# An earlier first weight chunk and moved conversions in a windowed-attention and two-MLP kernel

## The chip, the cores and the metric

The kernel runs on one core of one Trainium2 chip. The time is device microseconds of one execution, from launch to end. The kernel before took 948.12 us (median of 3 runs, 947.3 to 948.22). Five engines work side by side, each through its own instruction queue in order: TensorE (PE, with weight loads as PEld), VectorE (DVE), ScalarE (ACT), GpSimd (POOL) and SyncE (SP), which here only issues transfers. They wait for each other through semaphores.

## The reference

```python
# attention: q, k, v are (4, 8, 576, 64) f32; window 128, causal, ALiBi slopes per head
scores = (1 / sqrt(64)) * q @ k.T
mask = (rel >= 0) & (rel < 128)                 # rel = query position - key position
scores = where(mask, scores - slope[h] * abs(rel), -1e9)
attn = softmax(scores)                          # row sum + 1e-9 in the denominator
x = (attn @ v) with the heads of a token side by side      # (2304, 512)
# first MLP: w_in (512, 2048) and w_out (2048, 512), both float64
h = x @ w_in
g = where(h >= 1, h, where(h <= -1, 0, (h + 1)**2 / 4))
x = g @ w_out
# second MLP, same shapes, float64 weights
h = x @ w_in2
out = (h * clip(h + 3, 0, 6) / 6) @ w_out2
```

## The kernel before, in words

**Stages.** The 2304 tokens are cut into attention units of 64 to 256 tokens (`units`). A unit has 8 heads, and a head one or two blocks of up to 128 queries; one block of one head is a *step*. The first unit has 256 tokens, so 16 steps. The first MLP runs over blocks of 256 or 384 tokens and over 16 chunks of the hidden dimension (`f`), the second MLP after it. Attention steps of later units are dealt out between the first MLP's chunks; the first unit's run alone, ahead of everything.

**A step.** `Attention.tick` (L601) runs one step's stages at lags: `stage_a` (L414) makes the scores on TensorE (`s`, L411), VectorE takes bias, mask and row minimum (L441), and ScalarE the exponential (L445, `p` and `sm`). Two ticks later `stage_b` transposes on TensorE (`t`, L469 and L470) and ScalarE copies (`tt`). Three ticks later `stage_c_whole` multiplies with the values (`r`, L506). After both heads of a pair VectorE divides (`rec`, `y`, L518 to L520); a tick later `stage_d_whole` transposes (L531), ScalarE casts the chunk of `x` and VectorE writes its remainder (L152 and L159, both helper lines). A pair of heads gives one of the four 128-row chunks of x; the first MLP's hidden products (`h`, L655) need all four. `h` goes through VectorE (L684), ScalarE (L685), VectorE (L686), a cast on ScalarE (`g`, L152) and a remainder on GpSimd (`g`, L159) before `acc` (L697) can use it.

**Weights.** A chunk `f` of the float64 weights comes in two transfers of 512 KB, w_in and w_out (`Weights.load`, L172: one of the two each time it is called), into `rawa<f>`. It is turned into a pair of f32 tiles in three parts (L189 to L220): `conv1` has ScalarE on the two 32-bit halves (L194 and L198) and GpSimd on the sign (L197); `conv2` puts the parts together on VectorE (L205 and L212, both with two inputs in SBUF); `conv3` casts on ScalarE (`wa`, L152) and takes the remainder on VectorE (`wa`, L159). `conv_tick` (L222) emits `conv2` and `conv3` of chunk n-1 and then `conv1` of chunk n. The first hidden products of chunk f need `wa` of that chunk.

**Order.** SyncE's order is that of the program text. TensorE, VectorE, ScalarE and GpSimd are ordered when the program is built, by a scheduler that works with its own estimates; `tc.issue_after(i)` makes it put what is emitted inside behind instruction i, and `att.behind()` (L630) does so with the last step's row minimum. The pre-phase (L859 to L865) runs `n_pre` = 20 ticks: 16 of the first unit and four of lag, in which the first steps of the second unit start. Its only weight work are one load at every even tick and four calls of `conv_tick`, at t = 9, 14, 18 and 19. The first MLP then starts, with a hook per chunk (`spread`, L867) that calls one load, the conversions that are due, and the attention steps that are due.

Of the kernel before, what the change touches and what calls it, by code (L numbers as in the profile page):

```python
# [15 lines left out]
AF = mybir.ActivationFunctionType  # L16
# [17 lines left out]
LAG_B, LAG_C, LAG_D = 2, 3, 4  # L34
LAG_B_SPLIT, LAG_C_SPLIT = 3, 5
WARM_UP = 6
WHOLE = 4


@with_exitstack  # L40
def tile_window_attention_two_mlps(
# [15 lines left out]
    nc = tc.nc  # L57
# [190 lines left out]
    for j, (t0, n) in enumerate(units):  # L248
        for h in range(H):
# [9 lines left out]
            u.p = {}  # L259
            u.whole = j < WHOLE  # L260
            u.n_a = u.n_c = 0
# [8 lines left out]
    class Attention:  # L270
# [143 lines left out]
        def stage_a(self, n, i):  # L414
# [4 lines left out]
            nk = a + m - ks  # L419
# [9 lines left out]
            pt = self.pt[self.n_p % ((LAG_B if u.whole else LAG_B_SPLIT) + 1)]  # L429
            self.n_p += 1  # L430
            sm = self.work.tile([P, 4], F32, tag="sm", name=f"sm{n}_{i}", bufs=4)
# [3 lines left out]
            if not u.whole and a >= P:  # L435
# [3 lines left out]
                nk, table = P, self.near  # L439

            self.row = nc.vector.tensor_tensor_reduce(  # L441
                out=pt[:, :nk], in0=ps[:, :nk], in1=table,
                scale=-scale if u.whole else -slopes[u.h],
                scalar=3.0e38, op0=ALU.add, op1=ALU.min, accum_out=sm[:, 0:1])
            nc.scalar.activation(out=pt[:, :nk], in_=pt[:, :nk], func=AF.Exp, bias=sm[:, 0:1],  # L445
                                 scale=-1.0, accum_out=None if u.whole else sm[:, 1:2])
            if not u.whole:
                nc.vector.tensor_scalar(out=sm[:, 2:3], in0=sm[:, 1:2], scalar1=EPS, scalar2=None, op0=ALU.add)  # L448
# [152 lines left out]
        def tick(self):  # L601
            t = self.t
            self.t += 1
            first, whole = unit_steps[0], sum(unit_steps[:WHOLE])
            for lag, span, stage in ((LAG_D, range(first), self.stage_d_whole),
                                     (LAG_D + 1, range(first, whole), self.stage_d_whole),
                                     (LAG_C, range(whole), self.stage_c_whole),
                                     (LAG_C_SPLIT, range(whole, len(steps)), self.stage_c),
                                     (LAG_B, range(whole), self.stage_b),
                                     (LAG_B_SPLIT, range(whole, len(steps)), self.stage_b)):  # L610
                if t - lag in span:
                    stage(*steps[t - lag])
            if t < len(steps):
                n, i = steps[t]
                u = heads[n]
                self.more_loads(n + 3)
                self.more_preps(n)
                self.stage_a(n, i)
                late, self.late = self.late, []
                with self.behind():  # L620
                    for x in late:
                        self.to_x(*x)
                    if i == 0:
                        self.more_preps(n + 1 if u.whole or len(u.qbs) > 1 else n + 2)
                self.more_loads(n + 3)
            else:
                while self.late:
                    self.to_x(*self.late.pop(0))

        def behind(self):  # L630


            return tc.issue_after(self.row.ins) if self.row else ExitStack()
# [186 lines left out]
    W1 = Weights("a", w_in1, w_out1, cpool, True)  # L820
# [16 lines left out]
    with ExitStack() as actx:  # L837
# [6 lines left out]
        att = Attention(raw, proc, work, XX)  # L844
# [5 lines left out]
        bank = psum.tile([P, BANK], F32, tag="h1", name="busy")  # L850
        for _ in range(WARM_UP):
            keep_busy(bank, BANK)
# [2 lines left out]
            nc.gpsimd.memset(vt[:, :, 0:2 * D + 2:2 * D + 1], 1.0)  # L855
        att.more_loads(1)
        W1.load()

        n_pre = unit_steps[0] + LAG_D  # L859
        for t in range(n_pre):  # L860
            att.tick()
            if t % 2 == 0:
                W1.load()
            if t in (n_pre // 2 - 1, n_pre - 6) or t >= n_pre - 2:
                W1.conv_tick()  # L865

        def spread(part, ticks, conv):  # L867

# [467 lines left out]
```

## Time and profile before

| | us |
|---|---|
| median of 3 runs | 948.12 (947.3 to 948.22) |
| the profiled execution | 946.91 |
| its span, from the first to the last instruction | 945.2 |

| engine | busy us | share of the span | instructions |
|---|---|---|---|
| PE | 928.9 | 98% | 5683 |
| PEld | 875.2 | 93% | 5683 |
| DVE | 659.8 | 70% | 1750 |
| ACT | 535.4 | 57% | 1349 |
| POOL | 306.1 | 32% | 575 |

A line of the timeline gives an instruction's start and duration; the next instruction of the same engine can start some tenths of a microsecond before the one ahead has ended, so the start of the next one tells better what an instruction costs its engine. Matmuls overlap too, so a TensorE that reads as busy can still issue fewer matmuls than it could: the count in a stretch (x) says more. In square brackets stands how long the engine sat idle before the instruction and who ended it. Shares are averages over the whole program, whose first 60 us differ much from the rest.

### The profile page before, as it was taken

Reading aid. Unit: us, or ns where it says so; the run is one execution under the profiler, and the core shown is the slowest. Engines: PE = TensorE matmul, PEld = TensorE weight load, DVE = VectorE, ACT = ScalarE, POOL = GpSimd, SP = SyncE. Lnnn points to the kernel's source line nnn. Section 1 sums busy time; section 2 is a strip of 40 time slices with the busy share of each in tenths; the row PEclk is TensorE's granted clock in tenths of the full one; section 3 lists DMA queues with packets and bytes.
Section 4 is the critical chain, followed back from the end, with each engine's and each line's share of the span. In section 5 each row is a group of like instructions: output and inputs, shape, how many; then the busy total and the mean of one; then the engine's idle time right before and its main releaser. Section 6 shows DMA issues by size and latency. Waiting matters only on the chain.

```text
span 945.2 us, 17238 instructions
## 1 busy us (share of the span) xinstructions
PE 928.9 (98%) x5683; PEld 875.2 (93%) x5683; DVE 659.8 (70%) x1750; ACT 535.4 (57%) x1349; POOL 306.1 (32%) x575
## 2 busy tenths in 40 slices
PE   8899999999999999999999999999999999999998
PEld 6799999999999999999999999999999898888987
DVE  6998975786677677767647989848557777644443
ACT  6998854676667566666636876425333334423233
POOL 3243844787668676777710000000000000000000
PEclk9999999999999999999999999999999999999999
DMA  8858332232222212322007880004264644543441
GB/s 258 238 170 271 107 93 88 68 86 68 73 61 76 77 47 62 88 76 61 3 34 251 298 276 22 1 23 167 79 211 167 235 171 151 169 123 112 122 113 67
DMA packets 95337, 114.90 MB, mean 122 GB/s; under 512 B 8848, under 2 KB 73616, under 8 KB 95248
## 3 DMA queue, kind: packets, MB, share of 16 engines
q1 hardware_dynamic: 95248, 113.80, 38.2%
q8 instruction: 45, 0.74, 0.3%
q14 instruction: 44, 0.36, 0.1%
HBM read 88.60 MB, written 25.17 MB: 120 GB/s over the span
## 4 chain that ended last, share of the span: by engine, by line
PE 85%; DVE 6%; DMA 3%; ACT 3%; issue 1%; POOL 1%; SPq 0%; ACTq 0%; POOLq 0%; DVEq 0%
PE h L655 25%; PE acc L756 21%; PE acc L697 17%; PE y L1237 7%; PE x L1237 5%; PE s L411 3%; PE r L554 3%; DMA rawa<-w_out 2%; PE t L470 2%; PE r L506 1%; DMA rawa<-w_in 1%; DVE kl L391 1%; DVE r L684 1%; DVE r L686 1%; DMA qw<-qT 1%
## 5 line engine op out<-in xcount | busy, mean ns | idle before, releaser
L655 PE MATMUL h<-x,wa 128*128 128x384 f32 (+1 forms) x1344 | 231.0, 317 | 1.2 <-DVE r L686 0.8
L697 PE MATMUL acc<-g,wa 128*128 128x384 f32 (+1 forms) x1344 | 227.7, 315 | 0.4 <-POOL g L159 0.4
L756 PE MATMUL acc<-wb,g 128*128 128x512 f32 x861 | 222.2, 393 | 0.0
L655 PEld LDWEIGHTS h<-x,wa 128*128 128x128 f32 x1344 | 206.6, 189 | 4.3 <-DVE r L686 3.1
L697 PEld LDWEIGHTS acc<-g,wa 128*128 128x128 f32 x1344 | 206.2, 189 | 1.0 <-POOL g L159 0.6
L756 PEld LDWEIGHTS acc<-wb,g 128*128 128x128 f32 x861 | 159.4, 188 | 24.9
L152 ACT CAST g<-r 128x384 fp32r<-128x384 f32 (+1 forms) x208 | 101.3, 487 | 70.4 <-DVE r L1184 37.6
L159 POOL TENSOR_TENSOR g<-r,g 128x256 fp32r<-128x256 f32 (+1 forms) x96 | 93.4, 973 | 67.5 <-ACT g L152 51.4
L685 ACT ACTIVATE r<-r 128x384 f32<-128x384 f32 (+1 forms) x112 | 53.5, 478 | 80.4 <-DVE r L684 79.8
L159 DVE TENSOR_TENSOR g<-r,g 128x384 fp32r<-128x384 f32 x112 | 62.4, 557 | 43.2 <-ACT g L152 42.8
L684 DVE TENSOR_SCALAR r<-h 128x384 f32<-128x384 f32 (+1 forms) x112 | 55.4, 495 | 45.0 <-PE h L655 38.2
L488 POOL TENSOR_SCALAR_AFFINE_SELECT tt<-dist 128x256 fp32r<-128x256 f32 (+1 forms) x176 | 76.5, 455 | 14.0 <-DVE dist L483 13.9
L686 DVE TENSOR_TENSOR r<-h,r 128x384 f32<-128x384 f32 (+1 forms) x112 | 55.8, 499 | 27.9 <-ACT r L685 26.1
L655 PE MATMUL h<-x,wb 128*128 128x384 f32 x384 | 72.5, 336 | 0.0
L655 PEld LDWEIGHTS h<-x,wb 128*128 128x128 f32 x384 | 68.2, 188 | 2.6
L445 ACT ACTIVATE p<-p,sm 128x128 f32<-128x128 f32 (+2 forms) x134 | 57.0, 427 | 21.0 <-DVE sm L441 20.8
L1182 ACT ACTIVATE r<-u 128x384 f32<-128x384 f32 x32 | 16.8, 526 | 56.5 <-DVE u L1246 56.5
L554 PEld LDWEIGHTS r<-tt,vs 128*128 128x128 f32 x304 | 44.7, 189 | 3.1 <-issue 1.4
L393 POOL TENSOR_TENSOR qs<-qr,qs 128x256 fp32r<-128x256 f32 (+2 forms) x64 | 39.4, 616 | 25.1 <-ACT qs L390 13.3
L554 PE MATMUL r<-tt,vs 128*128 128x128 f32 (+3 forms) x304 | 44.3, 262 | 1.3 <-POOL tt L488 0.9
L470 PE MATMUL t<-ident,p 128*128 128x128 f32 x134 | 38.4, 288 | 1.0 <-DVE sm L448 0.5
L391 DVE SCALAR_TENSOR_TENSOR kl<-kr,kh 128x256 fp32r<-128x256 f32 (+3 forms) x64 | 38.9, 608 | 0.0
(161 smaller groups left out, 1553.6 us busy)
## 6 DMA issues: line engine op xcount, KB each, us to landing
w<-wd SPq DMA_DIRECT2D x88, 256.0 KB, 2.7
rawa<-w_in SPq DMA_DIRECT2D x16, 512.0 KB, 5.2
rawa<-w_out SPq DMA_DIRECT2D x16, 512.0 KB, 5.4
rawb<-w_in SPq DMA_DIRECT2D x16, 512.0 KB, 3.9
rawb<-w_out SPq DMA_DIRECT2D x16, 512.0 KB, 4.9
wd<-sum SPq DMA_DIRECT2D x32, 256.0 KB, 2.2
wd<-wb SPq DMA_DIRECT2D x24, 256.0 KB, 2.8
out<-o SPq DMA_DIRECT2D x17, 256.0 KB, 2.2
```

Source lines behind the costliest of these rows:

```text
L152: nc.scalar.copy(hi, x)
L159: engines[eng].tensor_tensor(out=lo, in0=x, in1=hi.bitcast(F32), op=ALU.subtract)
L445: nc.scalar.activation(out=pt[:, :nk], in_=pt[:, :nk], func=AF.Exp, bias=sm[:, 0:1], scale=-1.0, accum_out=None if u.whole else sm[:, 1:2])
L470: nc.tensor.transpose(ps[:, 1, :], pt[:, P:] if u.whole and has_prev else pt[:, :P], ident)
L488: nc.gpsimd.affine_select(out=u.tt[:, :, s0 + s, :m], in_=both, compare_op=ALU.is_ge, fill=0.0, base=-1 + s, pattern=[[0, 2], [sign, m]], ...
L554: nc.tensor.matmul(u.r[:, qo:qo + nq], u.vs[:, j, c, :, :].rearrange("p a d -> p (a d)"), u.tt[:, part].rearrange("p s q -> p (s q)")[:, s ...
L655: nc.tensor.matmul(ps[:, :n], self.W.w_in(a, c, f), self.x_chunk(x, b, c, n), start=(k == 0), stop=(k == 3 * KC - 1))
L684: nc.vector.tensor_scalar(out=r[:, :n], in0=ps[:, :n], scalar1=-1.0, scalar2=1.0, op0=ALU.max, op1=ALU.min)
L686: nc.vector.tensor_tensor(out=r[:, :n], in0=ps[:, :n], in1=r[:, :n], op=ALU.max)
L697: nc.tensor.matmul(acc[i][:, o * n:(o + 1) * n], self.W.w_out(a, f)[:, e * P:(e + 1) * P], g[:, b, :n], start=(first and k == 0 and o == 0 ...
L756: nc.tensor.matmul(acc[t][:, :DM], g[:, b, tg * P:(tg + 1) * P], self.W.w_out(a, f), start=(first and k == 0), stop=(last and k == 2))
L1237: nc.tensor.matmul(ps[:, :N2], w[:, a, c * P:(c + 1) * P], self.x.operand(k, c, b), start=(start and n == 0), stop=(n == 5), skip_group_ch ...
```

## The change

There are two parts. In front of the pre-phase `W1.load()` is called twice, not once, so the second half of chunk 0 is asked for right behind the first; each load of the pre-phase and of the hooks after it is then one transfer further than before. And the four calls of `conv_tick` stand at t = 4, 10, 15 and 19 in place of 9, 14, 18 and 19, inside a context that queues everything that they emit behind the last step's row minimum and its exponential.

```diff
--- before.py
+++ after.py
@@ -34,6 +34,7 @@
 LAG_B, LAG_C, LAG_D = 2, 3, 4
 LAG_B_SPLIT, LAG_C_SPLIT = 3, 5
 WARM_UP = 6
+CONV_AT = 4, 10, 15, 19
 WHOLE = 4
 
 
@@ -442,7 +443,7 @@
                 out=pt[:, :nk], in0=ps[:, :nk], in1=table,
                 scale=-scale if u.whole else -slopes[u.h],
                 scalar=3.0e38, op0=ALU.add, op1=ALU.min, accum_out=sm[:, 0:1])
-            nc.scalar.activation(out=pt[:, :nk], in_=pt[:, :nk], func=AF.Exp, bias=sm[:, 0:1],
+            self.exp = nc.scalar.activation(out=pt[:, :nk], in_=pt[:, :nk], func=AF.Exp, bias=sm[:, 0:1],
                                  scale=-1.0, accum_out=None if u.whole else sm[:, 1:2])
             if not u.whole:
                 nc.vector.tensor_scalar(out=sm[:, 2:3], in0=sm[:, 1:2], scalar1=EPS, scalar2=None, op0=ALU.add)
@@ -627,6 +628,9 @@
                 while self.late:
                     self.to_x(*self.late.pop(0))
 
+        def behind_exp(self):
+            return tc.issue_after(self.exp.ins)
+
         def behind(self):
 
 
@@ -855,14 +859,16 @@
             nc.gpsimd.memset(vt[:, :, 0:2 * D + 2:2 * D + 1], 1.0)
         att.more_loads(1)
         W1.load()
+        W1.load()
 
         n_pre = unit_steps[0] + LAG_D
         for t in range(n_pre):
             att.tick()
             if t % 2 == 0:
                 W1.load()
-            if t in (n_pre // 2 - 1, n_pre - 6) or t >= n_pre - 2:
-                W1.conv_tick()
+            if t in CONV_AT:
+                with att.behind(), att.behind_exp():
+                    W1.conv_tick()
 
         def spread(part, ticks, conv):
 
```

SyncE's queue behind the first weight transfer, before. `kw` is a head's k, `qw` a pair's q, `vr` a pair's v, `rawa0` weight chunk 0; the first pair's loads stand ahead of these rows.

```order
L182 DMA rawa0_169<-w_in1 128x4x256
L315 DMA kw1_106<-kT 64x256
L317 DMA qw0_107<-qT 128x256
L315 DMA kw1_106<-kT 64x256
L327 DMA vr1_103<-v 128x2x128
L186 DMA rawa0_169<-w_out1 128x1024
L315 DMA kw_kh0_109<-kT 64x256
L317 DMA qw1_108<-qT 128x256
L315 DMA kw_kh1_110<-kT 64x256
L327 DMA vr2_104<-v 128x2x128
L182 DMA rawa1_202<-w_in1 128x4x256
```

The same place after the change.

```order
L183 DMA rawa0_169<-w_in1 128x4x256
L187 DMA rawa0_169<-w_out1 128x1024
L316 DMA kw1_106<-kT 64x256
L318 DMA qw0_107<-qT 128x256
L316 DMA kw1_106<-kT 64x256
L328 DMA vr1_103<-v 128x2x128
L183 DMA rawa1_182<-w_in1 128x4x256
L316 DMA kw_kh0_109<-kT 64x256
L318 DMA qw1_108<-qT 128x256
L316 DMA kw_kh1_110<-kT 64x256
L328 DMA vr2_104<-v 128x2x128
```

The second half of chunk 0 went ahead of the second pair's k, q and v, and the first half of chunk 1 ahead of the third pair's; every later pair stands behind one more weight transfer in the same way.

ScalarE's queue from the exponential of step 4 on, before. `sm2_0` names head 2, block 0; `tt` are the copies of transposed probabilities, `x1` the cast of the first x chunk, `ma0` and `rawa0` the conversion of chunk 0.

```order
L445 ACTIVATE p1_114<-p1_114,sm2_0_225 128x128
L445 ACTIVATE p2_115<-p2_115,sm2_1_237 128x256
L445 ACTIVATE p0_113<-p0_113,sm3_0_258 128x128
L152 COPY tt2_247<-t2_0_248 128x128
L152 COPY tt2_247<-t2_1_270 128x256
L445 ACTIVATE p1_114<-p1_114,sm3_1_277 128x256
L152 CAST x_78<-x1_263 128x256
L194 ACTIVATE ma0_304<-rawa0_169 128x1024
L152 COPY tt3_282<-t3_0_283 128x128
L152 COPY tt3_282<-t3_1_294 128x256
L445 ACTIVATE p2_115<-p2_115,sm4_0_289 128x128
L198 ACTIVATE rawa0_169<-rawa0_169 128x1024
```

After the change.

```order
L446 ACTIVATE p1_114<-p1_114,sm2_0_226 128x128
L195 ACTIVATE ma0_231<-rawa0_169 128x1024
L199 ACTIVATE rawa0_169<-rawa0_169 128x1024
L446 ACTIVATE p2_115<-p2_115,sm2_1_243 128x256
L153 COPY tt2_253<-t2_0_254 128x128
L446 ACTIVATE p0_113<-p0_113,sm3_0_264 128x128
L153 COPY tt2_253<-t2_1_275 128x256
L153 CAST x_78<-x1_268 128x256
L446 ACTIVATE p1_114<-p1_114,sm3_1_282 128x256
L446 ACTIVATE p2_115<-p2_115,sm4_0_294 128x128
L153 COPY tt3_287<-t3_0_288 128x128
L446 ACTIVATE p0_113<-p0_113,sm4_1_307 128x256
```

Both conversion instructions of chunk 0 now stand next to each other right behind the exponential of head 2's first block, ahead of that of its second block; before, they stood seven and eleven places behind it. When ScalarE's queue comes to the exponential of head 8's first block (`sm8_0`), the same instructions stand ahead of it in both programs.

ScalarE's queue a little later, up to the cast of the fourth chunk of x (`x7`), before.

```order
L152 COPY tt8_450<-t8_0_451 128x256
L152 COPY tt8_450<-t8_1_483 128x256
L194 ACTIVATE ma3_497<-rawa3_329 128x1024
L445 ACTIVATE p0_113<-p0_113,sm9_0_461 128x256
L152 CAST wa2_494<-ma2_471 128x1024
L152 CAST x_78<-x7_475 128x256
L445 ACTIVATE p1_114<-p1_114,sm9_1_489 128x256
L198 ACTIVATE rawa3_329<-rawa3_329 128x1024
```

After the change.

```order
L153 COPY tt8_461<-t8_0_462 128x256
L153 COPY tt8_461<-t8_1_484 128x256
L446 ACTIVATE p0_113<-p0_113,sm9_0_472 128x256
L153 CAST x_78<-x7_476 128x256
L446 ACTIVATE p1_114<-p1_114,sm9_1_490 128x256
L195 ACTIVATE ma3_498<-rawa3_297 128x1024
L199 ACTIVATE rawa3_297<-rawa3_297 128x1024
L195 ACTIVATE ma4_529<-rawa4_370 128x1024
L153 CAST wa2_495<-ma2_427 128x1024
```

The cast of x7 and the exponentials of head 9 now stand ahead of chunk 3's first conversion (`ma3`) and of the cast of chunk 2 (`wa2`), which stood ahead of them before; behind them three conversion instructions stand in a row.

## Rows read from the trace of the kernel before

**Rows 1.** Busy time by stretch of 20 us; columns in the first line.
```profile
core 0: us, PE busy (x) PEld busy (x) DVE busy (x) ACT busy (x) POOL busy (x), PEclk, DMA share, GB/s
0.00:20.00 20.00, 16.39 (x104) 12.40 (x105) 11.73 (x45) 12.13 (x30) 6.12 (x22) 1.00 0.85 249
20.00:40.00 20.00, 16.01 (x110) 13.46 (x109) 17.69 (x41) 18.43 (x33) 6.85 (x7) 1.00 1.01 291
40.00:60.00 20.00, 19.36 (x148) 18.11 (x148) 19.32 (x48) 18.83 (x40) 6.88 (x8) 1.00 0.38 118
60.00:80.00 20.00, 20.00 (x171) 19.93 (x171) 17.31 (x52) 18.85 (x41) 9.77 (x17) 1.00 0.72 221
```

**Rows 2.** SyncE's timeline, 4 to 10 us: start us, duration us, then the transfer issued.
```profile
4.34 0.59 SPq L317 DMA_DIRECT2D qw<-qT  x1
...
6.12 0.47 SPq L186 DMA_DIRECT2D rawa<-w_out  x1
...
7.15 0.58 SPq L317 DMA_DIRECT2D qw<-qT  x1
...
9.44 0.50 SPq L186 DMA_DIRECT2D rawa<-w_out  x1
```

**Rows 3.** Transfers issued 3.3 to 6.5 us: count, size, us from issue to landing.
```profile
rawa<-w_out SPq DMA_DIRECT2D x1, 512.0 KB, 5.5
...
qw<-qT SPq DMA_DIRECT2D x1, 128.0 KB, 4.0
```

**Rows 4.** The same for transfers issued 6.7 to 9.9 us.
```profile
rawa<-w_out SPq DMA_DIRECT2D x1, 512.0 KB, 7.1
...
qw<-qT SPq DMA_DIRECT2D x1, 128.0 KB, 5.0
```

**Rows 5.** TensorE's timeline, 9.5 to 14.3 us: start us, duration us, instruction.
```profile
10.04 1.09 PE L411 MATMUL s<-kw,qw 128*128 128x128 f32 x6
...
13.73 0.39 PE L411 MATMUL s<-kw_kh,qw 128*128 128x128 f32 x2
```

**Rows 6.** VectorE's timeline, 10 to 11.2 us.
```profile
10.65 0.42 DVE L520 TENSOR_TENSOR y<-r,rec 128x256 f32<-128x256 f32 x1
10.99 0.28 DVE L441 CUSTOM_DVE_ANT_0 p<-s,dist 128x128 f32<-128x128 f32 x1
```

**Rows 7.** ScalarE's timeline, 11 to 39 us.
```profile
11.31 1.15 ACT L445 ACTIVATE p<-p,sm 128x128 f32<-128x128 f32 x3 [1.82 <-DVE sm L441]
...
13.62 1.15 ACT L194 ACTIVATE ma<-rawa 128x1024 f32<-128x1024 f32 x1
14.66 0.54 ACT L152 COPY tt<-t 128x128 f32<-128x128 f32 x2
...
15.38 1.19 ACT L198 ACTIVATE rawa<-rawa 128x1024 int32<-128x1024 uint32 x1
...
17.74 0.40 ACT L445 ACTIVATE p<-p,sm 128x128 f32<-128x128 f32 x1
...
28.38 0.54 ACT L445 ACTIVATE p<-p,sm 128x256 f32<-128x256 f32 x1
...
33.48 0.40 ACT L152 CAST x<-x 128x256 fp32r<-128x256 f32 x1
...
38.74 0.40 ACT L152 CAST g<-r 128x256 fp32r<-128x256 f32 x1
```

**Rows 8.** Busy time in two stretches, with the columns of rows 1.
```profile
11.31:18.05 6.74, 6.14 (x40) 4.36 (x39) 4.21 (x18) 6.28 (x16) 1.13 (x1) 1.00 1.06 322
18.05:38.74 20.69, 16.43 (x110) 13.62 (x111) 18.21 (x44) 18.74 (x35) 6.08 (x6) 1.00 1.00 288
```

**Rows 9.** VectorE's timeline, 42 to 52 us: one conversion step, twice.
```profile
42.86 1.22 DVE L212 CUSTOM_DVE_ANT_0 ma<-rawa,ma 128x2048 uint16<-128x2048 uint16 x1
...
49.29 2.17 DVE L212 CUSTOM_DVE_ANT_0 ma<-rawa,ma 128x2048 uint16<-128x2048 uint16 x1
```

**Rows 10.** GpSimd's timeline, 42 to 53 us.
```profile
49.26 1.15 POOL L197 TENSOR_SCALAR rawa<-rawa 128x1024 f32<-128x1024 f32 x1 [3.47 <-ACT ma L194]
```

## The prediction

> **What bounds the kernel now.** I read the busy time by stretch first. From 60 us on TensorE issues 171 matmuls in 20 us and is never idle; before that it issues 104, 110 and 148 [rows 1]. The first 20 us hold short padding matmuls and the start, so the stretches to look at are 20 to 40 (61 too few, at 20/171 = 0.117 us each some 7.1 us) and 40 to 60 (23, some 2.7 us). All that an edit of the start can win lies there, since afterwards TensorE sets the pace. In those 40 us ScalarE is busy for 18.43 + 18.83 = 37.26 us, VectorE for 37.01, and the transfers are saturated until 40 us (DMA share 0.85 and 1.01) [rows 1]. So the first 60 us belong to ScalarE and VectorE, who share attention steps and weight conversions, and behind them to the transfers. Second, SyncE's issues with the times to landing say when data is there [rows 2 to 4]; third, the timelines say who waited for it [rows 5 to 7].
>
> **The loads.** Before, the second half of chunk 0 lands at 6.12 + 5.5 = 11.6 us, q of the second pair at 4.34 + 4.0 = 8.3, q of the third at 7.15 + 5.0 = 12.15, the second half of chunk 1 at 9.44 + 7.1 = 16.5 [rows 2 to 4]. Transfers land in the order of issue and the engines are full, so bytes that are moved ahead delay those behind by their own time: 512 KB (0.524 MB) take 1.6 us at the 322 GB/s of a busy stretch [rows 8] and 2.1 at the 249 of the first [rows 1], in which this lies. I take 2.0. The second half of chunk 0 then lands near 9.8 us. The second pair's q lands at 10.4; its score matmul ran at 10.04 [rows 5], so it is 0.4 us late, but the row minimum behind it waited until VectorE had made y at 10.65 and started at 10.99 [rows 6]: hidden. The third pair's q lands near 14.15 and its scores ran at 13.73 [rows 5]: 0.4 us late, and its exponential is not due before 15.6 in the new order (below): hidden too, by ScalarE. If that cover were gone, the cost would be up to 0.6 us. Chunk 1 is complete at 16.6 as before, because the moved bytes are all ahead of it either way, and its conversion starts after that.
>
> **The conversions on ScalarE.** A long conversion instruction costs 14.66 - 13.62 = 1.04 us of ScalarE's queue [rows 7]. Chunk 0 would be there at 9.8, but its conversion is queued behind the exponential of step 4, which starts at 11.31 [rows 7] in both programs: the idle time ahead of 11.31 (1.82 us in that row) stays idle. The pair of conversions runs from 11.62 to 13.70, 2 us earlier than the first of them did (13.62), and the exponentials, copies and the first cast of x, which filled 11.62 to 13.62, follow it. What can be gained is ScalarE's idle time: 6.74 - 6.28 = 0.46 us between 11.31 and 18.05, and 20.69 - 18.74 = 1.95 between 18.05 and 38.74 [rows 8], 2.4 in all. I followed the new queue instruction by instruction with the durations of the trace. New waits appear, because the two or three engines of a step answer each other with less in flight: 0.5 us ahead of the exponential of head 4's second block, 0.8 ahead of the last copy of head 5, 0.35 ahead of head 8's copies, 0.65 ahead of the cast of x7, which comes to 2.3. So the queue is neither ahead nor behind: the exponential of head 5's first block ends at 17.6, where before two more copies (0.43 us) had been done by 18.05; and the exponential of head 8, with the same instructions ahead of it, starts at 28.3 (before 28.38 [rows 7]).
>
> **The fourth chunk of x.** From there the order differs in a way that helps. The first conversion of chunk 3 and the cast of chunk 2 (1.04 + 0.95 = 2.0 us) no longer stand ahead of the cast of x7, which moves from 33.48 [rows 7] to about 31.5. The first chunk's hidden products can end 2 us earlier. But its g does not come 2 us earlier: three conversion instructions now stand between, and I find its cast at 38.2 against 38.74 [rows 7], 0.54 us earlier, with 0.24 us more of other work done by then.
>
> **VectorE beside GpSimd.** The same conversion step took 1.22 us alone and 2.17 us where GpSimd's sign instruction began at the same time [rows 9, 10]. In the new order the sign instruction of chunk n starts when ScalarE has done the first conversion of chunk n, about when VectorE comes to that step of chunk n-1: near 18.7, 26.0 and 33.2 us. Each meeting costs VectorE between 0 and 0.95 us. VectorE was idle for 27.43 - 22.42 = 5.0 us of these two stretches [rows 8], which hides most; the one near 26 us delays the cast of chunk 1 by 0.5. The Trainium skill says the same under GPSIMD Engine Reference, section Specifications: GpSimd shares its SBUF interfaces with VectorE, with contention for VectorE instructions with two SBUF inputs, as this step is. By that rule all three meetings are paid in full, 2.85 us on VectorE, and if half a microsecond of each came through, the forecast would be 948.5 us.
>
> **The sum.** Loads 0; the earlier conversion 0; ScalarE's idle time 2.4 less new waits 2.3, within the next term; g earlier by 0.54 and 0.24 of work, 0.8; VectorE's meetings 0 to -0.8, taken as -0.3. That is -0.5 us. Later hooks call the same conversions at the same places, and the orders come together again within the first MLP's first blocks, so I carry the shift to the end unchanged. The profiled execution took 946.91 us (span 945.2), which becomes 946.4; the median of the runs lies 1.2 above it, so the forecast is 947.6 us. What a measurement can tell from no change is about 0.2%, 1.9 us: faster means below 946.2, slower above 950.0.
>
> **Rivals.**
> - *Faster: TensorE takes all of x7.* If the first hidden products end 2 us earlier and the later ones follow, the 7.1 us of missing matmuls shrink by that much and 0.5: 948.1 - 2.5 = 945.6, and up to 4 us if the new waits on ScalarE don't show. For it: hidden products are what TensorE lacks. Against: g's chain runs through ScalarE, which has the same work to do.
> - *Slower: the pair of conversions delays the first unit.* Two conversions, 2.08 us, stand ahead of the exponential of step 5, and each later step needs its answer from TensorE and VectorE. If ScalarE doesn't run back to back from 13.7 us on, that 2.08 us goes through to x7 and the first g, together with a late third pair: 948.1 + 2.1 = 950.2, to 951.5 with the 0.6 of the loads and VectorE's meetings. It decides from the point where the cast of x7 starts after 34.5. Against: ScalarE was idle for only 0.46 of the 6.74 us of that stretch [rows 8], so it had work in hand there.
> - *Nothing: it does not do what it says.* Chunk 0 is converted earlier, but chunk 1's tick is only one step earlier and the last tick is the same, so 2 us of head start end in the 40 to 60 us stretch, where ScalarE and VectorE are 94 and 97% busy [rows 1]: 948.1 to 949.
>
> **How the numbers follow.** Forecast 0.37 (its own range 946.4 to 948.6), nothing 0.16, faster 0.29 (943.9 to 946.2), slower 0.18 (949 to 951.5, a sixth of it under 950.0). Faster by over 0.2%: 0.29; within: 0.37 + 0.16 + 0.03 = 0.56; slower: 0.15. The range reaches into both outer cases and leaves out about a tenth at each end: 944.7 to 950.4.
>
> **What would show it.** SyncE's second transfer of chunk 0 landing before 10 us; ScalarE's pair of conversions at 11.6 to 13.7 right behind one exponential; the scores of the third pair near 14.3; the exponential of head 8 near 28.3; the cast of x7 near 31.5; the first g's cast near 38.2; VectorE's step at over 1.5 us near 18 or 26 us. The forecast is wrong if x7 comes at 31.5 or sooner and g's cast before 37.5 (faster), or if x7 comes after 33.5 (slower), or if stretches beyond 60 us, where I change nothing, issue another number of matmuls.

## The result, and the profile after

The changed kernel is slower: 957.49 us, median of 4 runs (955.86 to 958.02), where the kernel before took 947.87 on the same chip (947.3 to 948.22). The ratio is 1.0101 with a 95% interval of 1.0088 to 1.0113. The profiled execution took 957.05 us, its span 955.3, 10.1 more than before.

In the rows of after the line numbers are one higher as far as the attention goes (the conversions at L195 and L199 for L194 and L198, the helper at L153 for L152) and four higher in the MLP (L659 for L655). First the busy time by stretch, with the columns of [rows 1]; the last line is a stretch that rows 1 doesn't have.

```profile
0.00:20.00 20.00, 15.75 (x95) 12.31 (x95) 9.83 (x40) 11.32 (x27) 6.10 (x23) 1.00 0.91 270
20.00:40.00 20.00, 14.52 (x99) 11.70 (x97) 16.45 (x42) 17.34 (x34) 7.74 (x6) 1.00 0.92 272
40.00:60.00 20.00, 19.00 (x133) 17.53 (x133) 16.92 (x39) 17.38 (x36) 7.04 (x6) 0.91 0.42 134
60.00:80.00 20.00, 19.34 (x155) 18.57 (x154) 17.74 (x45) 18.00 (x36) 9.10 (x13) 1.00 0.52 160
...
120.00:140.00 20.00, 17.50 (x135) 17.50 (x136) 14.88 (x38) 10.73 (x29) 10.80 (x14) 0.91 0.23 70
```

Two things are new. TensorE's matmuls are fewer from 20 to 80 us (99, 133 and 155 for 110, 148 and 171), while over these 60 us ScalarE and VectorE are each busy for 3 us less, not for longer. And the granted clock, 1.00 in every stretch of before, reads 0.91 in two stretches. The same two stretches that [rows 8] shows, in the trace of after:

```profile
11.31:18.05 6.74, 4.99 (x35) 4.03 (x34) 2.90 (x16) 5.16 (x12) 1.09 (x1) 1.00 1.09 329
18.05:38.74 20.69, 15.77 (x111) 12.88 (x109) 17.14 (x44) 18.03 (x36) 6.79 (x6) 1.00 0.95 286
```

ScalarE does 5.16 + 18.03 = 23.19 us of work there, before 6.28 + 18.74 = 25.02; VectorE 20.04, before 22.42. By 38.74 us the one has 1.8 us of work less behind it and the other 2.4. ScalarE's timeline, answering to [rows 7], shows where that work has gone:

```profile
12.21 0.40 ACT L446 ACTIVATE p<-p,sm 128x128 f32<-128x128 f32 x1 [1.82 <-DVE sm L442]
12.52 1.12 ACT L195 ACTIVATE ma<-rawa 128x1024 f32<-128x1024 f32 x1
13.55 1.08 ACT L199 ACTIVATE rawa<-rawa 128x1024 int32<-128x1024 uint32 x1
...
30.08 0.52 ACT L446 ACTIVATE p<-p,sm 128x256 f32<-128x256 f32 x1
...
33.85 0.37 ACT L153 CAST x<-x 128x256 fp32r<-128x256 f32 x1 [0.64 <-PE x L532]
34.12 0.51 ACT L446 ACTIVATE p<-p,sm 128x256 f32<-128x256 f32 x1
34.53 1.15 ACT L195 ACTIVATE ma<-rawa 128x1024 f32<-128x1024 f32 x1
35.59 1.15 ACT L199 ACTIVATE rawa<-rawa 128x1024 int32<-128x1024 uint32 x1
36.63 1.10 ACT L195 ACTIVATE ma<-rawa 128x1024 f32<-128x1024 f32 x1
37.65 1.03 ACT L153 CAST wa<-ma 128x1024 fp32r<-128x1024 f32 x1
...
41.14 0.41 ACT L153 CAST g<-r 128x256 fp32r<-128x256 f32 x1 [0.46 <-DVE r L690]
```

The conversions of the last step stand behind the exponential at 34.12, and then four long instructions follow each other, where before they lay between the exponentials. The first event hangs on them. TensorE's timeline there:

```profile
36.17 0.48 PE L659 MATMUL h<-x,wa 128*128 128x256 f32 x2
39.12 0.70 PE L412 MATMUL s<-kw,qw 128*128 128x256 f32 x2 [2.46 <-DVE sm L442]
```

VectorE's:

```profile
37.49 1.23 DVE L206 SCALAR_TENSOR_TENSOR ma<-ma,rawa 128x1024 uint32<-128x1024 uint32 x1 [0.67 <-POOL rawa L198]
38.64 0.42 DVE L442 CUSTOM_DVE_ANT_0 p<-s,dist 128x256 f32<-128x256 f32 x1
```

GpSimd's:

```profile
35.76 1.70 POOL L198 TENSOR_SCALAR rawa<-rawa 128x1024 f32<-128x1024 f32 x1 [5.96 <-ACT ma L195]
```

Read backwards: the scores at 39.12 need the one score bank (the part of TensorE's result memory that scores go to), which the row minimum at 38.64 frees; that stands in VectorE's queue behind a conversion step of chunk 3, which waited 0.67 us for GpSimd's sign, which waited for ScalarE's conversion at 34.53. TensorE is idle for 2.46 us. Before, the scores at this place waited less than half as long:

```profile
38.10 0.70 PE L411 MATMUL s<-kw,qw 128*128 128x256 f32 x2 [1.09 <-DVE sm L441]
```

The second event is 80 us later. TensorE's timeline:

```profile
119.59 0.36 PE L701 MATMUL acc<-g,wa 128*128 128x256 f32 x1
122.50 2.06 PE L701 MATMUL acc<-g,wa 128*128 128x256 f32 x11 [2.54 <-POOL g L160]
```

GpSimd's:

```profile
116.62 3.07 POOL L160 TENSOR_TENSOR vs<-vr,vs 128x192 fp32r<-128x192 f32 x2
119.66 2.10 POOL L198 TENSOR_SCALAR rawa<-rawa 128x1024 f32<-128x1024 f32 x1
121.71 0.73 POOL L160 TENSOR_TENSOR g<-r,g 128x256 fp32r<-128x256 f32 x1
```

A g that TensorE needs at 119.96 stands on GpSimd behind 3.07 us of values and the sign of chunk 15. Behind each of the two waits the clock falls. The four stretches (wait, half clock, wait, half clock), with the columns of [rows 1]:

```profile
36.65:39.12 2.47, 0.01 (x2) 0.00 (x1) 1.80 (x5) 2.47 (x5) 2.11 (x2) 1.00 1.08 361
41.40:44.81 3.41, 3.41 (x17) 3.29 (x16) 2.37 (x7) 2.57 (x6) 1.20 (x1) 0.50 0.03 8
119.96:122.50 2.54, 0.00 (x1) 0.00 (x1) 0.84 (x2) 1.45 (x3) 2.54 (x3) 1.00 0.54 155
123.32:126.73 3.41, 3.41 (x19) 3.41 (x18) 2.96 (x4) 1.23 (x5) 2.98 (x4) 0.50 0.47 135
```

A granted clock of 0.50 is 1.2 GHz in place of 2.4. TensorE is busy throughout the two half-clock stretches, but they hold 17 and 19 matmuls, where 3.41 us at [rows 1]'s 171 in 20 us would hold 29.

How the 10 us add up is seen by putting the same matmuls of the first MLP's hidden products (`h`) of both traces side by side. The 19th starts at 35.56 (before 34.37, 1.2 late), the 37th, behind the first half-clock stretch, at 49.09 (44.66, 4.4 late), the 193rd at 117.51 (111.95, 5.6 late), the 217th, behind the second, at 129.00 (119.15, 9.9 late). From there to the end the lag is 9.5 to 10.1.

### The profile page after: what moved, and what is told of

Read it like the earlier page. It is cut to its first block, busy times and chain, and to the rows that moved or that the text cites. A ratio compares the mean times of both kernels' runs of the same rounds, so it can differ in the third digit from the quotient of the medians.

```text
span 955.3 us, 17233 instructions
## 1 busy us (share of the span) xinstructions
PE 933.7 (98%) x5683; PEld 879.0 (92%) x5683; DVE 661.3 (69%) x1750; ACT 535.4 (56%) x1349; POOL 307.4 (32%) x575
## 4 chain that ended last, share of the span: by engine, by line
PE 82%; DVE 5%; ACT 2%; DMA 2%; issue 1%; POOL 1%; SPq 0%; ACTq 0%; POOLq 0%; DVEq 0%
PE h L659 24%; PE acc L760 21%; PE acc L701 17%; PE y L1243 7%; PE x L1243 5%; PE r L555 3%; PE s L412 3%; PE t L471 1%; DMA rawb<-w_out 1%; DMA rawa<-w_out 1%; DVE r L688 1%; DVE kl L392 1%; PE r L507 1%; DVE ma L206 1%; DVE r L690 0%
## 5 line engine op out<-in xcount | busy, mean ns | idle before, releaser
L659 PE MATMUL h<-x,wa 128*128 128x384 f32 (+1 forms) x1344 | 233.6, 319 | 1.2 <-DVE r L690 0.7
L659 PEld LDWEIGHTS h<-x,wa 128*128 128x128 f32 x1344 | 208.8, 191 | 4.0 <-DVE r L690 2.9
L153 ACT CAST g<-r 128x384 fp32r<-128x384 f32 (+1 forms) x208 | 101.2, 487 | 70.4 <-DVE r L1190 37.6
L659 PE MATMUL h<-x,wb 128*128 128x384 f32 x384 | 72.4, 336 | 0.0
L659 PEld LDWEIGHTS h<-x,wb 128*128 128x128 f32 x384 | 68.2, 188 | 2.6
```

The lines of the kernel that those rows point to most:

```text
L153: nc.scalar.copy(hi, x)
L659: nc.tensor.matmul(ps[:, :n], self.W.w_in(a, c, f), self.x_chunk(x, b, c, n), start=(k == 0), stop=(k == 3 * KC - 1))
```

## Experiments

**Which part costs: six kernels with other combinations of the three parts.** The parts are the early load (a second `W1.load()`), the new steps (4, 10, 15, 19) and the queueing (`with att.behind(), att.behind_exp()`). The first four:

The changed kernel less the early load:

```diff
         W1.load()
-        W1.load()
```


> The changed kernel without the second early load: the conversions stay at the new steps and behind the exp and the row minimum. Theory A (the queueing puts the conversions of chunks 2 to 4 in one block ahead of step 20's row minimum, TensorE waits some 2.5 us at 39 us and runs 3.4 us at the lower clock behind it; later GpSimd stands late with a g at 119 us and the same follows): here the order ahead of step 20 has the row minimum behind the same two VectorE conversions, so the first wait stays and costs 4 to 6 us; near chunk 15 GpSimd's order is that of the kernel before, so the second need not come; 952 to 958 us. Theory B (the early load pushes the pairs' transfers back and is the cause): within 2 us of the before kernel, 946 to 950. Theory C (the moved steps put conversions ahead of the first unit's exps): slow as the changed kernel, 955 to 958.

The kernel before with the early load alone:

```diff
         W1.load()
+        W1.load()
```


> The kernel before with the second early load only: old steps, no queueing. Theory A: no block of conversions, no half-clock stretch near 41 us, 945 to 950 us. Theory B (the load is the cause): 955 to 958 us. Theory C (moved steps): 945 to 950 us.

The changed kernel less the queueing:

```diff
-                with att.behind(), att.behind_exp():
-                    W1.conv_tick()
+                W1.conv_tick()
```


> The changed kernel without the queueing behind exp and row minimum: moved steps and the early load stay. Theory A: conversions fall between the exps again, TensorE's wait at 39 us is under 1.5 us and its clock stays full; 945 to 950 us. Theory B (the load): 955 to 958 us. Theory C (moved steps): 955 to 958 us.

The changed kernel with the old steps:

```diff
-CONV_AT = 4, 10, 15, 19
+CONV_AT = 9, 14, 18, 19
```


> The changed kernel with the conversions at the old steps 9, 14, 18 and 19, queued behind exp and row minimum, with the early load. Theory A: three ScalarE conversions in a row and the row minimum of step 20 behind VectorE's, as in the changed kernel: TensorE waits about 2.5 us near 39 us and the clock falls to half behind it; 953 to 958 us. Theory B (the load): 955 to 958 us. Theory C (moved steps): 945 to 950 us.

Later, the new steps alone (no early load, no queueing), and the queueing alone (the old steps, one load):

> The kernel before with its conversions at the new steps 4, 10, 15 and 19, no second early load and no queueing. From the four combinations run, the early load alone costs 2.2 us and early load with the steps 1.1 us, so if the two add, the steps alone gain 1 us: 945.5 to 947.5 us. If the steps only gain with the early load (chunk 0 lands later without it), 947 to 950 us.

> The kernel before with the queueing behind exp and row minimum only: old steps 9, 14, 18 and 19, one early load. If the queueing is the part that loses wherever it stands: 954 to 960 us, a TensorE wait of 2 us or more near 40 us and a half-clock stretch behind it. If it loses only together with the early load (which lets the schedule ask for the conversions sooner): 947 to 950 us.

Measured, with the ratio to before and its interval; the last two columns are of the profiled execution alone: when ScalarE starts chunk 3's first conversion, and how long the granted clock was at half between the warm-up and the end.

| steps | loads | queued | median us | ratio | chunk 3 starts | half clock us |
|---|---|---|---|---|---|---|
| old | 1 | no (before) | 947.87 | 1 | 31.10 | 0 |
| old | 1 | yes | 956.89 | 1.0103 (1.0088 to 1.0118) | 37.08 | 10.2 |
| old | 2 | no | 949.80 | 1.0019 (1.0008 to 1.0029) | 30.08 | 0 |
| old | 2 | yes | 959.49 | 1.0128 (1.0113 to 1.0143) | 36.79 | 10.2 |
| new | 1 | no | 955.64 | 1.0082 (1.0070 to 1.0095) | 31.80 | 6.8 |
| new | 1 | yes | 953.23 | 1.0065 (1.0044 to 1.0087) | 36.32 | 13.7 |
| new | 2 | no | 948.70 | 1.0014 (1.0005 to 1.0024) | 28.68 | 0 |
| new | 2 | yes (after) | 957.49 | 1.0101 (1.0088 to 1.0113) | 34.53 | 6.8 |

The queueing alone is enough for the whole loss: 1.03% on the kernel before, and about 0.9 to 1.1% in two of the other three pairs. In the fourth (new steps, one load) it does not: there the kernel is 0.8% slower without it already. (The queued kernel of that pair also spreads widely, from 951.15 to 956.83 us over five executions.) So the early load as cause falls, and so does a simple sum of parts. Two expectations missed altogether: the new steps alone, which I had at 945.5 to 950, and the old steps with load and queueing, which came out above every range. The new steps cost 8 us where the second half of chunk 0 is asked for late: it lands at 10.80 us in that trace, and ScalarE converts it at 13.74 us, amid the first unit. They cost nothing where it is early: it lands at 9.32 us and is converted at 9.40, ahead of the exponential. That this place is the reason is my reading; no run tests it. The queueing alone has the first event too, and longer. Its TensorE timeline:

```profile
42.96 0.70 PE L412 MATMUL s<-kw,qw 128*128 128x256 f32 x2 [2.94 <-DVE sm L442]
```

The busy times of the stretch behind it, with the granted clock at 0.50:

```profile
44.04:50.87 6.83, 6.44 (x28) 6.26 (x29) 6.58 (x14) 4.08 (x8) 2.31 (x2) 0.50 0.49 133
```

In the profiled executions of this table every kernel that lost over 0.3% has half-clock stretches, and none of the others has one. In their other executions, of which only the mean granted clock is on record, the line is less sharp: it is 0.997 in two of eight of the early load alone, and 0.996 and 0.998 in two of ten of the kernel without the queueing. The kernel with the new steps alone shows that this needs no single long wait: ahead of the following stretch its TensorE timeline has no idle time over 0.6 us, only several smaller ones between 15 and 20 us. The busy times of that stretch:

```profile
19.71:26.54 6.83, 6.51 (x27) 5.73 (x27) 4.54 (x13) 5.48 (x11) 2.33 (x4) 0.50 0.79 234
```

**Which queueing: VectorE's or ScalarE's.** `att.behind()` holds back VectorE's part, `att.behind_exp()` ScalarE's.

```diff
-                with att.behind(), att.behind_exp():
+                with att.behind_exp():
```


> The changed kernel, its conversions queued behind the exp alone, not behind the row minimum. Theory A (VectorE's part: conversions of chunks 2 and 3 stand ahead of step 20's row minimum, and TensorE waits for the score bank that this row minimum frees): here no conversion stands right ahead of that row minimum, so TensorE waits under 1.5 us near 37 us, its clock stays full there, 947 to 952 us. Theory D (ScalarE's part: behind the exp the conversions start late and bunch into 3 to 4 us of ScalarE, whatever VectorE's order): the bunch is still there, 953 to 958 us.

```diff
-                with att.behind(), att.behind_exp():
+                with att.behind():
```


> The changed kernel, its conversions queued behind the row minimum alone, not behind the exp. Theory A: two first passes, two second passes and a weight remainder stand ahead of step 20's row minimum on VectorE, more than in the changed kernel, so the TensorE wait near 39 us is 2.5 us or more, 953 to 959 us. Theory D: ScalarE's conversions lie between the exps again, 947 to 951 us.

Measured: behind the exponential alone 954.27 us, ratio 1.0079 (1.0063 to 1.0094); behind the row minimum alone 951.26, 1.0041 (1.0027 to 1.0055). Theory A falls as the whole cause: with no conversion ahead of step 20's row minimum the wait of 2.46 us at 39 us is gone, and the kernel still loses 7 us. TensorE waits in another place, for the activation:

```profile
42.01 2.56 PE L659 MATMUL h<-x,wa 128*128 128x256 f32 x12 [1.54 <-DVE r L690]
```

and the half clock follows from 42.48 us on. In this kernel ScalarE starts chunk 3 at 37.64. The second kernel has a wait as long as the changed kernel's, though for the first g and not for the score bank:

```profile
39.77 0.50 PE L701 MATMUL acc<-g,wa 128*128 128x256 f32 x2 [2.98 <-ACT g L153]
```

Half clock follows from 40.57 to 43.98 us. Theory A's sign is there, and its price of 953 to 959 is not: with such a wait and 3.41 us at half clock this kernel is only 2.6 us slower than the one without queueing. So a wait of that length with its half clock does not make the loss by itself. Theory D, ScalarE's late and bunched conversions, names the larger part (954.27, within its 953 to 958), and the row minimum adds to it. D's price for the second kernel was 947 to 951, so its 951.26 is just outside.

**Which step, and how late a point.** Four kernels: the queueing at 4, 10 and 15 but not 19; at 19 only; at 4 only; and at all four, behind the exponential of one step earlier.

```diff
-                with att.behind(), att.behind_exp():
-                    W1.conv_tick()
+                if t == CONV_AT[-1]:
+                    W1.conv_tick()
+                else:
+                    with att.behind(), att.behind_exp():
+                        W1.conv_tick()
```


> The changed kernel, with the queueing at steps 4, 10 and 15 but not at step 19 (the last conversion before the first block). Both A and D put the loss at the last conversions, which here lie between the exps: 948 to 952 us, no half-clock stretch at 41 us. If the loss has built up over the earlier three steps (a share of about 2 us each), 953 to 956 us.

> The changed kernel with the queueing at step 19 only; the conversions of steps 4, 10 and 15 are free. Freed at step 19 alone it was 952.2 us, free everywhere 948.7. If the last step's queueing holds the two waits and the half-clock stretches (5 us) and the earlier three the rest: 952 to 956 us with a half-clock stretch near 41 us. If the loss needs the earlier three to be late as well: 948 to 950 us.

> The changed kernel with the queueing at step 4 only. If the lateness of 3 to 5 us that the kernel freed at step 19 shows without any half-clock stretch comes from the first pair of conversions (done 3 us later behind the exp of step 4 than without queueing): 951 to 953 us. If it comes from steps 10 and 15: 948 to 950 us.

```diff
         def behind_exp(self):
-            return tc.issue_after(self.exp.ins)
+            return tc.issue_after(self.last_exp.ins)
```


> The changed kernel, its conversions queued behind the exp of one step earlier (and behind the row minimum as in the change). If the loss is that the point behind which they stand comes late, so that VectorE and ScalarE stand idle between 8 and 38 us and the backlog comes due at 35 to 45 us: 949 to 953 us, VectorE's busy time in 8 to 38 us over 20.5 us against 19.9. If any queueing behind an exp is as bad: 954 to 958 us.

Measured: last free 952.17 us (ratio 1.0050, 1.0035 to 1.0065); last only 952.83 (1.0058, 1.0037 to 1.0080); first only 953.86 (1.0066, 1.0049 to 1.0083); one step earlier 954.19 (1.0073, 1.0059 to 1.0086). Over the 948.70 without queueing the first three steps cost 3.5 us, the first alone 5.2 (above both of its ranges), and all four 8.8: the steps don't add, and the first is not harmless, as I had left open. The last alone is 4.1 in the median, but its six executions lie in two groups, three at 950.1 to 951.1 with a mean granted clock of 0.998 to 1.0, and three at 954.6 to 955.9 with 0.992 to 0.995; so that median means little, and the same program is some 5 us longer where the clock falls more. With the last step free no half-clock stretch is left in the profiled execution, so those 3.5 us are lateness alone. The one-step-earlier kernel is a miss: VectorE's busy time from 8 to 38 us is 22.18 us, as the theory of idle time asked for (19.89 in after), and it still loses, by what comes behind 38 us: waits of 1.84 and 1.47 us and 6.8 us at half clock. Idle time before 38 us is thus not the only way to lose.

**The clock.** Dummy matmuls (zeros, into a free bank) fill the first wait:

```diff
+            if self.W is W1 and self.n_first == 2:
+                bank = psum.tile([P, BANK], F32, tag="acc1", name="fill")
+                with tc.issue_after(last.ins):
+                    for _ in range(FILL):            # 20
+                        self.fill = keep_busy(bank, 2 * P)
```


> The changed kernel plus 20 dummy matmuls (zeros, 256 columns, into a bank that is free) put into TensorE's queue where it waits 2.46 us at 36.7 to 39.1 us. The wait stays, as busy time. If the half-clock stretch of 3.41 us behind it belongs to the idle wait, it is gone and with it about 1.7 us: 954.5 to 956.5 us, and the later stretch at 123 us may stay or go. If the clock falls for another reason, it falls again and the time is 957 to 958 us.

Measured: 953.16 us, ratio 1.0071 (1.0046 to 1.0097), 4.3 less than the changed kernel. No half-clock stretch follows the filled wait. The profiled execution, at 957.7 us, had half clock at another place, from 15.9 and from 22.7 us; the other three took 952.5 to 953.5 with a mean granted clock of 0.999 to 1.0. The gain is over the 1.0 to 3.0 us that I had expected because the later stretch goes too: the wait for g, at 125 us here, is 1.44 us, not 2.54, and the clock stays full behind it. The edit moved more than it was meant to. The dummy matmuls read the tile `zeros`, which a later mask is built in, so three short instructions for that mask went to a later place (on GpSimd from 23.3 to 43.7 us, on VectorE from 24.6 to 113.3), and from 113 us on a few instructions of ScalarE and GpSimd stand elsewhere. ScalarE's order up to 112 us and TensorE's, but for the dummy matmuls, are the same. For the first stretch that leaves little but the filled wait; why the second wait shrank is not shown by this run.

**The second event by itself.** Chunk 15's sign is taken from GpSimd to VectorE; then both edits together:

```diff
-            if self.sign_pool:
+            if self.sign_pool and f != 15:
```


> The changed kernel, with the sign pass of chunk 15 taken off GpSimd (VectorE does that chunk's sign in its own second way, one pass more). If TensorE's wait of 2.54 us at 119.6 to 122.5 us is for that sign, which stands 2.10 us ahead of a g on GpSimd, the wait shrinks under 0.7 us and the half-clock stretch behind it (3.41 us) does not come: 952 to 954.5 us. If the wait is the phase in which GpSimd's whole queue of 116 to 123 us arrives, it stays and the time is 956 to 958 us.

> The changed kernel with both disturbances of the clock taken away: 20 dummy matmuls in TensorE's wait at 37 to 39 us, and chunk 15's sign on VectorE instead of GpSimd. Alone the first gave 953.2 us in its undisturbed runs and the second 954.1, of 957.5. If each half-clock stretch costs its own 1.7 us and the waits the rest, both together come to 950 to 952.5 us with no half-clock stretch before the end; what then remains over the kernel without queueing (948.7) is lateness without the clock, 2 to 4 us. If the two are one effect (the second follows from the first), 952.5 to 954 us.

Measured: the sign alone 954.07 us, ratio 1.0080 (1.0062 to 1.0099); both 951.54, 1.0043 (1.0028 to 1.0058). With the sign moved the wait shrinks from 2.54 to 1.45 us, not under 0.7: the g still stands behind 3.06 us of values on GpSimd. TensorE's timeline:

```profile
121.14 1.58 PE L701 MATMUL acc<-g,wa 128*128 128x256 f32 x11 [1.45 <-POOL g L160]
```

The half-clock stretch behind it is gone. Up to the sign itself this kernel has the changed kernel's order on all engines. With both edits TensorE's timeline has the dummy matmuls where the wait was:

```profile
35.94 0.48 PE L660 MATMUL h<-x,wa 128*128 128x256 f32 x2
36.27 2.36 PE L127 MATMUL fill<-zeros 128*128 128x256 bf16 x20
38.91 0.70 PE L413 MATMUL s<-kw,qw 128*128 128x256 f32 x2 [0.28 <-DVE sm L443]
```

and by its busy times the clock is full in both places:

```profile
40.00:45.00 5.00, 4.71 (x37) 4.52 (x38) 4.89 (x10) 4.05 (x10) 1.90 (x2) 1.00 0.24 73
...
120.00:125.00 5.00, 5.00 (x43) 5.00 (x43) 5.00 (x12) 3.86 (x10) 3.67 (x5) 1.00 0.61 167
```

This splits the loss. Of the 9.6 us between before and after, 957.49 - 951.54 = 6.0 go with the two events: two half-clock stretches of 3.41 us, which cost half of that each where they stand (the 37th matmul of the hidden products is 2.7 us late here, 4.4 in after), and the wait at 120 us, which in this kernel does not come. The split is not exact: by the 193rd the lag is 4.8 us here and 5.6 in after, so 0.8 of the first 1.7 us is left by then, and TensorE has a wait of 1.04 us at 111.77 us that after does not have. The other 4 us are lateness with the clock at full. Most of it is not repaid: the lag is 4.8 us at the 217th and 4.0 at the end.

**A version without the queueing and with the sign moved**, in case it beats the kernel before:

```diff
-                with att.behind(), att.behind_exp():
-                    W1.conv_tick()
+                W1.conv_tick()
...
-            if self.sign_pool:
+            if self.sign_pool and f != 15:
```


> The changed kernel without the queueing, and with chunk 15's sign on VectorE. Without the sign on VectorE it was 948.7 us, with a TensorE wait of 1.41 us at 116 us for a g that stands behind that sign on GpSimd. If the sign there is what the wait is for: 1 to 1.5 us less, 947 to 948 us, equal to the kernel before or slightly under it. If the g waits on its own chain: 948.5 to 949.5 us.

Measured: 948.39 us, ratio 1.0017 (1.0008 to 1.0026). The wait is shorter. TensorE's timeline with the sign on GpSimd, the third kernel of this section:

```profile
116.06 1.57 PE L701 MATMUL acc<-g,wa 128*128 128x256 f32 x11 [1.41 <-POOL g L160]
```

and with it on VectorE:

```profile
115.34 1.57 PE L701 MATMUL acc<-g,wa 128*128 128x256 f32 x11 [0.37 <-POOL g L160]
```

The time is that of the kernel with the sign on GpSimd (1.0014), not the 947 to 948 that I expected, so that 1 us did not reach the end. Nor is half clock always as dear as in after. Six of this kernel's eleven executions have a mean granted clock of 0.996 and take 947.99 to 949.68 us, median 948.4, where the two at 0.999 and 1.0 take 947.85 and 947.41. A mean lower by 0.003 is 2.8 us of clock lost in 947, and less than 1 us of it shows in the time. With two executions on one side this is a hint only, and where these falls lie is not on record, since the profiled execution has none. No kernel of this study beats the one before.

## Why the prediction was wrong

I forecast 947.6 us and no measurable change; it is 957.5 and above the range's end of 950.4. Point by point:

- *The loads* came much as forecast: chunk 0's second half landed at 9.05 us (below 10), the third pair's q at 12.68, sooner than the 14.15 I had. Chunk 1 was complete at 14.63 us, not at the 16.6 that I took as unchanged. That they cost nothing was off by some 2 us: the early load alone gives 1.0019.
- *The pair of conversions* stands right behind the exponential of step 4, at 12.52 to 14.6 and not 11.6 to 13.7, because that exponential starts at 12.21 in this execution. In the profiled executions of four other kernels that have the same order up to there (the last step free, the exponential alone, the sign moved, the dummy matmuls) it starts at 11.47 to 12.74, so I take this for an offset of the execution, not of the change.
- *"So the queue is neither ahead nor behind"* is the step that failed first. I took ScalarE's idle time of 2.4 us less new waits of 2.3. In the two stretches of [rows 8] the idle time did not shrink from 2.41 us to 2.3 but grew to 27.43 - 23.19 = 4.24, a difference of 1.8; VectorE's grew by 2.4. My reading is that what was queued behind an exponential could no longer fill the gaps ahead of it; the kernel with the exponential of one step earlier shows that this is not all of it, since it has VectorE busy for 22.18 us from 8 to 38 us (before 22.68, after 19.89) and loses as well. The exponential of head 8 starts at 30.08 (I said 28.3), x7's cast at 33.85 (31.5), the first g's at 41.14 (38.2). The text said that x7 after 33.5 would show it wrong on the slower side.
- *"Three conversion instructions now stand between"* is where I stopped one queue short. I followed those conversions along ScalarE to the first g and found it earlier. I did not follow them through GpSimd's sign to VectorE, whose conversion step stands ahead of step 20's row minimum, nor that row minimum to TensorE's only score bank: 2.46 us idle.
- *The clock* is no term of the sum, neither in the forecast nor in a rival. The granted clock of [rows 1] reads 1.00 throughout, and I took that for a property of the kernel. In after it fell behind each of the two long waits of TensorE; the experiments put 3.4 us on the two stretches. The Trainium skill (TensorE: Matmul & The Clock Gate, section HAM oscillation) tells of a kernel whose TensorE waits for a transfer between its bursts of matmuls: the wait puts it back to the lower clock, and the next burst starts there. The traces agree in part. With dummy matmuls in the wait the stretch behind it is gone; but the matmuls behind the wait that ended at 39.12 us started at full clock, and the fall came at 41.40.
- *"I carry the shift to the end unchanged"* failed at 120 us. I argued that the orders come together again, but a lag of 5.6 us was left at the 193rd matmul, and 4.3 us more were lost there. That the lag meets GpSimd's queue in another phase is my reading; what the runs show is that without the sign on GpSimd the wait is 1.45 us, not 2.54, and no half clock follows. The text named another number of matmuls beyond 60 us as a sign of being wrong: 155 for 171 from 60 to 80 us, 135 for 172 from 120 to 140.
- *VectorE beside GpSimd*: the three meetings came, but VectorE did not pay, so the term of -0.3 us measured 0 on VectorE. Its step took 1.22 us at 19.49, 27.60 and 35.28, and GpSimd's sign beside it 1.72, 1.95 and 1.70, where the first sign, alone, took 1.09. The price came round all the same: the sign of the third meeting ended some 0.6 us later than it would have alone, and VectorE's next step waited 0.67 us for it, ahead of the row minimum of the first event. Of the rule that the prediction took from the Trainium skill (GPSIMD Engine Reference, section Specifications) the trace shows the contention, here on the other of the two engines. That VectorE pays in full was my own addition. The 948.5 us that the prediction gives by that rule is also summed wrongly: 1.5 us in place of 0.3 makes 948.8.

Of the rivals, the slower one had the sign right and the wrong place: x7's cast came before its point of 34.5 us, and the loss is not the first pair's 2.1 us. Something of its kind exists all the same: the queueing at step 4 alone is 5.2 us slower than no queueing. Its profiled execution has 13.7 us at half clock, so the clock is part of it; this was not taken apart.

What stays open: how the 4 us of lateness come about and divide over the four queued steps, since one alone costs as much as three; and why the new steps need the early load, beyond the place where the conversion of chunk 0 lands in ScalarE's order.

## What to carry to other kernels

Before work is queued behind a late instruction to keep it out of the way, ask which idle gaps it has been filling: here ScalarE, 92% busy from 20 to 40 us before the change, did not make up for them, and the backlog came due where the next stage starts. Follow a bunch of moved instructions through every engine that handles them, to the buffer that TensorE needs next. And where a change can leave TensorE waiting for some microseconds, put a price on the clock too: here two waits of 2.5 us each cost about 1.7 us more than themselves. Look at more than one execution for it, since the same program can lose its clock in one and keep it in the next.

## What the runs showed of the hardware

- The clock's fall comes with a delay and is not proportional to one wait. In after it fell at 41.40 us, 2.3 us behind the end of a wait of 2.46, and at 123.32, 0.8 us behind the end of one of 2.54; behind the exponential alone it fell 0.5 us behind the end of a wait of 1.54; in the kernel with the new steps alone it fell with no wait over 0.6 us; and in the kernel without queueing it stayed full through waits of 1.43, 1.30 and 1.32 us within 15 us.
- It differs between executions of one program: with the dummy matmuls one of four lost it before 30 us, at 957.7 us, and three kept it, at 952.5 to 953.5.
- GpSimd's sign over 128x1024 takes 1.09 to 1.20 us alone, and VectorE's steps over a chunk 1.18 to 1.26. Where they meet, the one that began later pays, by about the time that both run. In after VectorE's step at 35.28 us was ahead of GpSimd's sign, and the sign took 1.70 us (the first line is of VectorE's timeline, the second of GpSimd's):

```profile
35.28 1.22 DVE L213 CUSTOM_DVE_ANT_0 ma<-rawa,ma 128x2048 uint16<-128x2048 uint16 x1
35.76 1.70 POOL L198 TENSOR_SCALAR rawa<-rawa 128x1024 f32<-128x1024 f32 x1 [5.96 <-ACT ma L195]
```

At 78 us the sign was ahead, and VectorE's step took 2.10 (GpSimd's line first):

```profile
78.24 1.13 POOL L198 TENSOR_SCALAR rawa<-rawa 128x1024 f32<-128x1024 f32 x1 [0.56 <-ACT ma L195]
78.35 2.10 DVE L213 CUSTOM_DVE_ANT_0 ma<-rawa,ma 128x2048 uint16<-128x2048 uint16 x1
```

[rows 9, 10] are of the second kind: the sign began at 49.26 us, the step at 49.29. Over the traces of all kernels here I counted the meetings of just one step and one sign that overlap by more than 0.3 us. In the 55 where VectorE began first, its step kept 1.19 to 1.23 us and the sign took 0.97 to 1.04 more than the overlap; in the 16 where the sign began first, it kept 1.11 to 1.19 and VectorE's step took 1.06 to 1.09 more than the overlap. The sign of the second event is one more of the first kind: it took 2.10 us because VectorE's step, at 119.52, was 0.14 us ahead of it.
